# The routing's logits, taken from the transposed rows as stationary operand

## The chip, the core and the metric

The kernel runs on one core of a Trainium2 chip, as one program. The metric is the device time of the whole program in microseconds (us); the median of three runs is given with the lowest and the highest. PE is the TensorE matmul engine, PEld its loads of the stationary operand, DVE is VectorE, ACT is ScalarE, POOL is GpSimd, SP is SyncE.

## What is computed

Three stages follow one another; only the second contains the change. B = 4 batches, H = 8 heads, 768 positions, head dimension 48, so 3072 tokens of 384 numbers.

```
# 1 linear attention with a decaying state, per batch and head
for t in range(S):
    cur = einsum('bhd,bhe->bhde', u * k_t, v_t)
    y[:, :, t] = einsum('bhd,bhde->bhe', r_t, state + cur)
    state = w * state + einsum('bhd,bhe->bhde', k_t, v_t)
# 2 a mixture of 8 experts, each token goes to one
xn = x / (norm(x) + 1e-6);  en = emb / (norm(emb) + 1e-6)
logits = xn @ en.T / tau
e = argmax(logits);  gate = softmax(logits)[e]
out[mask_e] = gate * (relu(x[mask_e] @ w1[e]) @ w2[e])      # 384 -> 1024 -> 384
# 3 a dense feed-forward over all tokens, 384 -> 2048 -> 384
h = x @ w_in;  out = (h * clip(h + 3, 0, 6) / 6) @ w_out
```

## The kernel before

**Attention.** The sequence is cut into six chunks c of 128 positions, and the heads into four pairs hp. The loop runs over the 24 groups (c, hp), all four batches in each. In one group DVE scales the transposed r and k by tables (`r_s` L625, `k_s` L624), PE forms the scores `a_ps` (L632), ACT copies them to `a_m` and POOL masks them (L636). POOL also forms `ku`, the product of r, k and u (L640, L641); DVE sums it to `a_t` (L648) and multiplies v by it (`av`, L663). `kk` (L652) feeds `u_ps` (L660), from which DVE updates the state (L686). `y_ps` (L667, L671) is copied to `y_sb` and transposed back into `x_ps` (L690), and DVE adds `av` and writes the token rows `x_t` (L691). `x_t` has two buffers of 128 positions x 4 batches x 388, one per chunk; so chunk 5 writes the buffer from which chunk 3 was scattered.

**Routing.** `route(c)` treats the 512 tokens of a chunk once `x_t` is whole. It is a generator in four steps, taken one or two at a time between the groups of the next chunk. In step one, 12 transposes (L223) and three copies on ACT make `xT`, the rows with the 384 numbers on the partitions, and ACT sums the squares (L228). In step two, three matmuls (L233) have the normalised expert directions `enT` as stationary operand (8 columns, padded to 32 per block of 128) and 512 tokens moving; ACT copies `lt_ps` to `lt`. `inv_norm` (L201 to L214, 14 short DVE instructions) gives 1/norm. In step three, four transposes (L240) bring the logits back to one token per partition; DVE sums the three blocks (L242), takes the maximum (L245), subtracts it (L246), finds the first index at the maximum (L248 to L251), forms the one-hot `ohot` and `aft` (L254, L256), scales by 1/norm (L257), and ACT takes the exponential `ex` (L259). In step four, PE counts with triangular and all-ones matrices (`r_ps`, `c_ps`, L263 to L271), DVE reads the rank (L273, L275), the destination `dsti` (L277), the gate (L279 to L281, written into column 384 of `x_t`) and the running counts (L282, L283); POOL then issues four indirect scatters (L286), each of 128 rows of `x_t` to `xs_d` in memory.

All of the routing's PSUM tiles, and those of the experts' transposes, share one pool `psM` with two buffers. After chunk 2, `leader` (L339 to L349, with L325 as its last instruction) picks the expert with most tokens so far; its first 256 rows are gathered from `xs_d` (L385), and its weights are split into high and low parts (L189, L192).

**After the attention.** The expert with most tokens runs first. The routing of chunk 5 stands among its matmuls (L410 to L412, `mm3`) in an order fixed by `pin = tc.keep_in_program_order`. Its scatters, the final order of the experts and the gathers of the other experts follow. Everywhere else the order on an engine is not written out: a scheduler of the framework places instructions by its own model of when their inputs are ready. An engine runs its instructions strictly in the order so found.

Of the kernel before, what the change touches and what calls it, by code (L numbers as in the profile page):

```python
# [8 lines left out]
F32 = mybir.dt.float32  # L9
# [6 lines left out]
ALU = mybir.AluOpType  # L16
AX = mybir.AxisListType
# [4 lines left out]
B, H, S, D = 4, 8, 768, 48  # L22
NT = B * S
DM = H * D
KD = DM // 128
E, F1, F2 = 8, 1024, 2048
# [18 lines left out]
def rwkv_moe_kernel(ctx, tc, dT, tokA, wT, uw, emb, tau, w1, w2, win, wout, out):  # L45
    nc = tc.nc
    wide = win.dtype == I64

    const = ctx.enter_context(tc.tile_pool(name="const", bufs=1))
# [5 lines left out]
    psM = pctx.enter_context(tc.tile_pool(name="psM", bufs=2, space=PSUM))  # L55
# [12 lines left out]
    ident = const.tile([128, 128], F32, name="ident")  # L68
# [32 lines left out]
    start = const.tile([128, E], F32, name="start")  # L101
# [17 lines left out]
    lead_f = const.tile([128, 4], F32, name="lead_f")  # L119
    lead_i = const.tile([128, 2], I32, name="lead_i")  # L120
    n0 = lead_f[:, 1:2]
    enT = const.tile([128, KD, 32], F32, name="enT")
    nc.gpsimd.memset(enT, 0.0)


    w_src = []
# [82 lines left out]
    def inv_norm(pool, ss, shape, nm):  # L209

        y = rsqrt_newton(pool, ss, shape, nm)
        nc.vector.tensor_tensor(out=y, in0=y, in1=ss, op=ALU.mult)
        nc.vector.tensor_scalar(out=y, in0=y, scalar1=1e-6, scalar2=None, op0=ALU.add)
        nc.vector.reciprocal(out=y, in_=y)  # L214
        return y

    def route(c, x_t, sm, xT, st_p, group="rows", pin=lambda i: i):
# [10 lines left out]
            nc.scalar.activation(out=junk, in_=x_t[:, b, 0:DM], func=AF.Square, accum_out=ss[:, b:b + 1])  # L228
        yield

        lt_ps = psM.tile([KD * 32, B, 128], F32, name="lt_ps", tag="m")
        for k in range(KD):
            pin(nc.tensor.matmul(lt_ps[k * 32:k * 32 + 32], lhsT=enT[:, k, :], rhs=xT[:, k], start=True, stop=True))  # L233
        lt = sm.tile([KD * 32, B, 128], F32, name="lt", tag="lt")
        nc.scalar.copy(out=lt, in_=lt_ps)
        rn = inv_norm(sm, ss, [128, B], "n")
        yield
        l_ps = psM.tile([128, B, KD, 32], F32, name="l_ps", tag="m")
        for b in range(B):
            pin(nc.tensor.transpose(l_ps[:, b].rearrange("p k e -> p (k e)"), lt[:, b, :], ident[0:KD * 32, 0:KD * 32]))  # L240
        lg = sm.tile([128, B, E], F32, name="lg", tag="lg")
        nc.vector.tensor_reduce(out=lg, in_=l_ps[:, :, :, 0:E].rearrange("p b k e -> p b e k"), axis=AX.X, op=ALU.add)  # L242

        mx = sm.tile([128, B], F32, name="mx", tag="mx")
        nc.vector.tensor_reduce(out=mx, in_=lg, axis=AX.X, op=ALU.max)  # L245
        nc.vector.tensor_tensor(out=lg, in0=lg, in1=mx.unsqueeze(2).to_broadcast([128, B, E]), op=ALU.subtract)  # L246
        sel = sm.tile([128, B, E], F32, name="sel", tag="sel")
        nc.vector.tensor_scalar(out=sel, in0=lg, scalar1=0.0, scalar2=float(E), op0=ALU.is_lt, op1=ALU.mult)  # L248
        nc.vector.tensor_tensor(out=sel, in0=sel, in1=iot, op=ALU.add)
# [276 lines left out]
    with actx:  # L526
# [3 lines left out]
        sm = actx.enter_context(tc.tile_pool(name="sm", bufs=2))  # L530
# [43 lines left out]
        while n < C:  # L574
            nc.vector.tensor_tensor(out=ptab[:, :, n + 1:2 * n + 1], in0=ptab[:, :, 1:n + 1],
                                    in1=ptab[:, :, n:n + 1].to_broadcast([112, HP, n]), op=ALU.mult)
# [22 lines left out]
        def directions():  # L599

            emj = st_p.tile([128, DM], BF16, name="junk", tag="junk")[0:E, :]
            ess = st_p.tile([E, 1], F32, name="ess")
            nc.scalar.activation(out=emj, in_=em, func=AF.Square, accum_out=ess)
            ern = inv_norm(st_p, ess, [E, 1], "e")
            nc.vector.reciprocal(out=ta, in_=ta)
            nc.vector.tensor_scalar(out=em, in0=em, scalar1=ern, scalar2=ta, op0=ALU.mult, op1=ALU.mult)
            eps = psM.tile([128, KD, E], F32, name="eps", tag="m")
            for k in range(KD):
                nc.tensor.transpose(eps[:, k, :], em[:, k * 128:(k + 1) * 128], ident[0:E, 0:E])
            nc.vector.tensor_copy(enT[:, :, 0:E], eps)  # L610

        state = []
        for hp in range(HP):
# [91 lines left out]
        for i, (c, hp) in enumerate(groups):  # L705
# [9 lines left out]
            if i == 1:  # L715
                directions()
            if i == HP:
                range_flag()
            if hp == HP - 1 and c < NCH - 1:
                pend = route(c, x_t, sm, xp.tile([128, KD, B, 128], F32, name="xT", tag="xT", bufs=1), st_p)  # L720
# [21 lines left out]
        psC = pctx.enter_context(tc.tile_pool(name="psC", bufs=1, space=PSUM))  # L742
        pin = tc.keep_in_program_order
        last_r = route(NCH - 1, x_t, sm, xp.tile([128, KD, B, 128], F32, name="xT", tag="xT", bufs=1), st_p, pin=pin)
        step(last_r, 1)

# [133 lines left out]
    with ExitStack() as mctx:  # L880
        m1 = mctx.enter_context(tc.tile_pool(name="m1", bufs=1))

        def again():
# [44 lines left out]
            for c in range(NCH):  # L928
                x_t = m1.tile([128, B, DG], F32, name="x_t", tag="x")
                xT = stg.tile([128, WCH], F32, name="xT", tag="wst").rearrange("p (k b t) -> p k b t", k=KD, b=B)  # L930
                nc.gpsimd.memset(x_t[:, :, DM + 1:DG], 0.0)
                nc.sync.dma_start(out=x_t[:, :, 0:DM], in_=y_d.rearrange("(b c p) d -> c p b d", b=B, p=C)[c])
                for f in step(route(c, x_t, m1, xT, m1, "rows_again"), 4):
                    f()
# [208 lines left out]
```

## Time and profile before

| | us |
|---|---|
| median of 3 runs (lowest, highest) | 876.92 (872.75, 880.08) |
| the profiled execution | 870.2 |
| its span, first to last instruction | 868.5 |
| PE busy | 820.0 |
| DVE busy | 523.3 |
| ACT busy | 347.3 |
| POOL busy | 262.7 |

The mean granted TensorE clock of the profiled execution is 0.944 of full speed. Busy times are sums over the whole span; the engines run side by side. The attention with the routing of chunks 0 to 4 takes the first 200 us, the first expert with the routing of chunk 5 follows, and all after that is expert and feed-forward work. "Idle before" in a row is the time an engine stood still before the instruction, with what ended it. The granted clock is given as a share of 2.4 GHz, 0.50 being 1.2 GHz.

### The profile page before, as it was taken

To read this page: it belongs to the slowest core of one execution; us is meant where nothing else is said; L and a number is where in the kernel's file an instruction comes from. 1 tells how busy PE (TensorE), PEld (TensorE's weight loads), DVE (VectorE), ACT (ScalarE), POOL (GpSimd) and SP (SyncE) were. 2 spreads that over 40 slices of the span, in tenths; PEclk is the share of its full clock that TensorE was granted. 3 is DMA by queue.
4 is the path that set the end of the run, shared out by engine and by line. 5 is a ranking of instruction groups with operands and counts; after the bars stand their busy time and mean duration, and the time that the engine had idled before them with its cause. 6 is when DMAs were issued, how large, how long until landed. Compare 5 with 4: busy or idle time off the path is not lost. (4 is left out here: it accounts for less than half of the span.)

```text
span 868.5 us, 13312 instructions
## 1 busy us (share of the span) xinstructions
PE 820.0 (94%) x5005; PEld 729.0 (84%) x5006; DVE 523.3 (60%) x1105; ACT 347.3 (40%) x668; POOL 262.7 (30%) x280
## 2 busy tenths in 40 slices
PE   7998997979999999997898999999999999999994
PEld 5876785758899999997888888898998899988983
DVE  8478989977387877782546888744334334333331
ACT  3443343543544554452544433343333334333331
POOL 7646656755323322647210211121002002001001
PEclk8587888899999999999899999999999999999997
DMA  7434536713465656562222221111001001001001
GB/s 219 146 130 157 173 131 207 263 65 119 151 215 173 204 180 208 189 197 81 94 93 61 69 66 62 37 37 37 1 1 37 0 1 37 1 1 37 0 1 37
DMA packets 25083, 85.09 MB, mean 98 GB/s; under 512 B 4780, under 2 KB 7009, under 8 KB 25008
## 3 DMA queue, kind: packets, MB, share of 16 engines
q1 hardware_dynamic: 19072, 69.44, 24.9%
q0 software_dynamic: 5936, 14.70, 4.8%
q8 instruction: 42, 0.69, 0.3%
q14 instruction: 33, 0.27, 0.1%
HBM read 71.47 MB, written 12.64 MB: 97 GB/s over the span
## 5 line engine op out<-in xcount | busy, mean ns | idle before, releaser
L410 PE MATMUL l<-xh,whi 128*128 128x512 f32 (+8 forms) x504 | 184.9, 372 | 4.1 <-DVEq L1009 3.1
L411 PE MATMUL l<-xl,whi 128*128 128x512 f32 (+8 forms) x504 | 187.1, 372 | 1.2 <-issue 1.2
L412 PE MATMUL l<-xh,wlo 128*128 128x512 f32 (+8 forms) x504 | 186.6, 371 | 0.9 <-issue 0.9
L446 DVE SCALAR_TENSOR_TENSOR rg<-rg,l 128x512 f32<-128x512 f32 x96 | 65.7, 686 | 132.7 <-ACT rg L445 125.2
L445 ACT ACTIVATE rg<-l,three 128x512 f32<-128x512 f32 x96 | 65.8, 689 | 166.4 <-PE l L412 154.9
L461 PE MATMUL o<-wlo,hh 128*128 128x384 f32 x384 | 128.6, 335 | 0.4 <-POOL wlo L1039 0.4
L460 PE MATMUL o<-whi,hh 128*128 128x384 f32 x384 | 128.0, 336 | 0.5 <-ACT hh L447 0.5
L462 PE MATMUL o<-whi,hl 128*128 128x384 f32 x384 | 124.2, 335 | 0.0
L412 PEld LDWEIGHTS l<-xh,wlo 128*128 128x128 f32 x504 | 95.8, 190 | 15.1 <-issue 2.2
L410 PEld LDWEIGHTS l<-xh,whi 128*128 128x128 f32 x504 | 95.3, 190 | 15.2 <-issue 4.7
L411 PEld LDWEIGHTS l<-xl,whi 128*128 128x128 f32 x504 | 95.6, 190 | 11.3 <-issue 1.1
L1069 POOL DMA_INDIRECT out_dram<-o_t,ctok x20 | 20.9, 1043 | 254.1 <-ACT o_t L1067 250.5
L448 DVE TENSOR_TENSOR hl<-rg,hh 128x512 fp32r<-128x512 f32 x96 | 66.4, 693 | 43.5 <-ACT hh L447 42.1
L447 ACT CAST hh<-rg 128x512 fp32r<-128x512 f32 x96 | 59.5, 621 | 75.1 <-DVE rg L446 60.4
L507 DVE SCALAR_TENSOR_TENSOR hl<-l,hh 128x256 fp32r<-128x256 f32 (+7 forms) x72 | 38.1, 541 | 69.7 <-ACT hh L506 53.8
L460 PEld LDWEIGHTS o<-whi,hh 128*128 128x128 f32 x384 | 72.0, 188 | 5.2 <-ACT hh L447 0.8
L461 PEld LDWEIGHTS o<-wlo,hh 128*128 128x128 f32 x384 | 72.1, 188 | 4.3 <-POOL wlo L1039 0.7
L506 ACT ACTIVATE hh<-l 128x256 fp32r<-128x256 f32 (+7 forms) x72 | 33.6, 481 | 103.2 <-PE l L412 63.3
L411 PE MATMUL acc<-hl,whi 128*128 128x256 f32 (+7 forms) x216 | 72.0, 335 | 0.5 <-issue 0.2
L412 PE MATMUL acc<-hh,wlo 128*128 128x256 f32 (+7 forms) x216 | 72.4, 336 | 0.0
L462 PEld LDWEIGHTS o<-whi,hl 128*128 128x128 f32 x384 | 71.7, 188 | 0.3
L410 PE MATMUL acc<-hh,whi 128*128 128x256 f32 (+7 forms) x216 | 65.1, 335 | 0.1
(216 smaller groups left out, 1332.6 us busy)
## 6 DMA issues: line engine op xcount, KB each, us to landing
wst<-in_w_dram SPq DMA_DIRECT2D x32, 768.0 KB
tk<-in_tok_dram SPq DMA_DIRECT2D x24, 576.0 KB
dt_t<-in_dT_dram SPq DMA_DIRECT2D x24, 448.0 KB
q<-in_win_dram SPq DMA_DIRECT2D x16, 384.0 KB
q<-in_wout_dram SPq DMA_DIRECT2D x16, 384.0 KB
wf_d<-t SPq DMA_DIRECT2D x16, 192.0 KB
wst<-wf_d SPq DMA_DIRECT2D x4, 768.0 KB
rows<-xs_d,prod POOLq DMA_INDIRECT x27
```

Source lines behind the costliest of these rows:

```text
L410: pin(nc.tensor.matmul(ps, lhsT=w[0], rhs=x[0], start=first, stop=False))
L411: pin(nc.tensor.matmul(ps, lhsT=w[0], rhs=x[1], start=False, stop=False))
L412: pin(nc.tensor.matmul(ps, lhsT=w[1], rhs=x[0], start=False, stop=last))
L445: nc.scalar.activation(out=r6, in_=ps, func=AF.Relu, bias=three)
L446: nc.vector.scalar_tensor_tensor(out=gf, in0=r6, scalar=6.0, in1=ps, op0=ALU.min, op1=ALU.mult)
L447: nc.scalar.copy(out=gh, in_=gf)
L448: nc.vector.tensor_tensor(out=gl, in0=gf, in1=gh.bitcast(F32), op=ALU.subtract)
L460: pin(nc.tensor.matmul(acc[t], lhsT=gh[:, sl], rhs=wh[:, f % 4, :], start=(f == span[0]), stop=False))
L461: pin(nc.tensor.matmul(acc[t], lhsT=gh[:, sl], rhs=wl[:, f % 4, :], start=False, stop=False))
L462: pin(nc.tensor.matmul(acc[t], lhsT=gl[:, sl], rhs=wh[:, f % 4, :], start=False, stop=(f == span[1] - 1)))
L506: last["a"] = nc.scalar.activation(out=hh[:, 0:n], in_=ps[:, 0:n], func=AF.Relu).ins
L507: last["v"] = nc.vector.scalar_tensor_tensor(out=hl[:, 0:n], in0=ps[:, 0:n], scalar=0.0, in1=hh[:, 0:n].bitcast(F32), op0=ALU.max, op1=ALU ...
```

## The change

`enT` loses its padding and is [128, 3, 8]; the memset of the padded tile goes. In step two of `route`, the logits are formed by 12 matmuls per chunk: for each batch b and each block k of 128 numbers, `xT[:, k, b]` (128 x 128) is the stationary operand and `enT[:, k]` (8 columns) moves; the three blocks add up in PSUM. `l_ps` therefore has tokens on the partitions at once. The three matmuls L233, the copy to `lt`, the four transposes L240 and the sum L242 are gone. The maximum and the subtraction read `l_ps` from PSUM and stand at the end of step two, ahead of `inv_norm` in the program. What follows is as before. Line numbers in the text are those of before; those of the changed file are 7 lower from L246 on (1 lower in `inv_norm`), and its own maximum and subtraction are L236 and L237.

```diff
--- before.py
+++ after.py
@@ -119,8 +119,7 @@
     lead_f = const.tile([128, 4], F32, name="lead_f")
     lead_i = const.tile([128, 2], I32, name="lead_i")
     n0 = lead_f[:, 1:2]
-    enT = const.tile([128, KD, 32], F32, name="enT")
-    nc.gpsimd.memset(enT, 0.0)
+    enT = const.tile([128, KD, E], F32, name="enT")
 
 
     w_src = []
@@ -228,22 +227,16 @@
             nc.scalar.activation(out=junk, in_=x_t[:, b, 0:DM], func=AF.Square, accum_out=ss[:, b:b + 1])
         yield
 
-        lt_ps = psM.tile([KD * 32, B, 128], F32, name="lt_ps", tag="m")
-        for k in range(KD):
-            pin(nc.tensor.matmul(lt_ps[k * 32:k * 32 + 32], lhsT=enT[:, k, :], rhs=xT[:, k], start=True, stop=True))
-        lt = sm.tile([KD * 32, B, 128], F32, name="lt", tag="lt")
-        nc.scalar.copy(out=lt, in_=lt_ps)
+        l_ps = psM.tile([128, B, E], F32, name="l_ps", tag="m")
+        for b in range(B):
+            for k in range(KD):
+                pin(nc.tensor.matmul(l_ps[:, b], lhsT=xT[:, k, b], rhs=enT[:, k], start=(k == 0), stop=(k == KD - 1), skip_group_check=True))
+        lg = sm.tile([128, B, E], F32, name="lg", tag="lg")
+        mx = sm.tile([128, B], F32, name="mx", tag="mx")
+        nc.vector.tensor_reduce(out=mx, in_=l_ps, axis=AX.X, op=ALU.max)
+        nc.vector.tensor_tensor(out=lg, in0=l_ps, in1=mx.unsqueeze(2).to_broadcast([128, B, E]), op=ALU.subtract)
         rn = inv_norm(sm, ss, [128, B], "n")
         yield
-        l_ps = psM.tile([128, B, KD, 32], F32, name="l_ps", tag="m")
-        for b in range(B):
-            pin(nc.tensor.transpose(l_ps[:, b].rearrange("p k e -> p (k e)"), lt[:, b, :], ident[0:KD * 32, 0:KD * 32]))
-        lg = sm.tile([128, B, E], F32, name="lg", tag="lg")
-        nc.vector.tensor_reduce(out=lg, in_=l_ps[:, :, :, 0:E].rearrange("p b k e -> p b e k"), axis=AX.X, op=ALU.add)
-
-        mx = sm.tile([128, B], F32, name="mx", tag="mx")
-        nc.vector.tensor_reduce(out=mx, in_=lg, axis=AX.X, op=ALU.max)
-        nc.vector.tensor_tensor(out=lg, in0=lg, in1=mx.unsqueeze(2).to_broadcast([128, B, E]), op=ALU.subtract)
         sel = sm.tile([128, B, E], F32, name="sel", tag="sel")
         nc.vector.tensor_scalar(out=sel, in0=lg, scalar1=0.0, scalar2=float(E), op0=ALU.is_lt, op1=ALU.mult)
         nc.vector.tensor_tensor(out=sel, in0=sel, in1=iot, op=ALU.add)
@@ -607,7 +600,7 @@
             eps = psM.tile([128, KD, E], F32, name="eps", tag="m")
             for k in range(KD):
                 nc.tensor.transpose(eps[:, k, :], em[:, k * 128:(k + 1) * 128], ident[0:E, 0:E])
-            nc.vector.tensor_copy(enT[:, :, 0:E], eps)
+            nc.vector.tensor_copy(enT, eps)
 
         state = []
         for hp in range(HP):
```

The scheduler places the attention's instructions anew. Three places follow, before and after, with the line numbers of each file.

On POOL, at the end of the attention: `ku` is the product that DVE's `a_t` sums, `a_m` the mask, the DMA rows the scatters of a chunk. Before:

```order
L640 TENSOR_TENSOR ku<-tk,ubc 128x384
L641 TENSOR_TENSOR ku<-ku,tk 128x384
L640 TENSOR_TENSOR ku<-tk,ubc 128x384
L636 AFFINE_SELECT a_m<-a_m 128x512 x2
L641 TENSOR_TENSOR ku<-ku,tk 128x384
L286 DMA xs_d<-x_t,dsti 3072x388 x4
L636 AFFINE_SELECT a_m<-a_m 128x512 x2
L711 MEMSET x_t 128x4x3
```

The scatters are those of chunk 3; the `ku` products of the last two groups of the attention (two multiplications each) stand ahead of them. After:

```order
L634 TENSOR_TENSOR ku<-ku,tk 128x384
L279 DMA xs_d<-x_t,dsti 3072x388 x4
L633 TENSOR_TENSOR ku<-tk,ubc 128x384
L629 AFFINE_SELECT a_m<-a_m 128x512 x2
L634 TENSOR_TENSOR ku<-ku,tk 128x384
L704 MEMSET x_t 128x4x3
L633 TENSOR_TENSOR ku<-tk,ubc 128x384
L629 AFFINE_SELECT a_m<-a_m 128x512
L634 TENSOR_TENSOR ku<-ku,tk 128x384
L629 AFFINE_SELECT a_m<-a_m 128x512
L633 TENSOR_TENSOR ku<-tk,ubc 128x384
L634 TENSOR_TENSOR ku<-ku,tk 128x384
```

The scatters of chunk 3 now stand ahead of the `ku` products of the last three groups.

On DVE, the same chunk 3 between its gate and its destination rows. Before:

```order
L691 TENSOR_TENSOR x_t<-x_ps,av 128x4x96
L648 TENSOR_REDUCE a_t<-ku 128x8
L279 TENSOR_REDUCE gate<-ex 128x4
L663 TENSOR_TENSOR av<-tk,a_t 128x384
L280 TENSOR_SCALAR gate<-gate 128x4
L281 RECIPROCAL x_t<-gate 128x4
L648 TENSOR_REDUCE a_t<-ku 128x8
L273 TENSOR_TENSOR at<-r_ps,ohot 128x32
L282 TENSOR_TENSOR cum<-c_ps,cum 128x8
L283 TENSOR_TENSOR delta<-c_ps,cum 128x8
L275 TENSOR_REDUCE rank<-at 128x4
L277 TENSOR_SCALAR dsti<-rank 128x4
```

Here the gate (L279 to L281) stands ahead of `dsti` (L277), with the two last `a_t` of the attention among them. After, from `dsti` on:

```order
L270 TENSOR_SCALAR dsti<-rank 128x4
L641 TENSOR_REDUCE a_t<-ku 128x8
L273 TENSOR_SCALAR gate<-gate 128x4
L274 RECIPROCAL x_t<-gate 128x4
L617 TENSOR_TENSOR k_s<-dt_t,itab 112x512
L684 TENSOR_TENSOR x_t<-x_ps,av 128x4x96
L679 SCALAR_TENSOR_TENSOR state_0_229<-state_1_230,ptab,u_ps 48x4x48 x2
L656 TENSOR_TENSOR av<-tk,a_t 128x384
L618 TENSOR_TENSOR r_s<-dt_t,ptab 112x512
L641 TENSOR_REDUCE a_t<-ku 128x8
L684 TENSOR_TENSOR x_t<-x_ps,av 128x4x96
L617 TENSOR_TENSOR k_s<-dt_t,itab 112x512
```

Behind `dsti` (now L270) and the reciprocal (now L274, the other input of the scatters) stand `k_s`, `x_t`, two state updates, `av` and `r_s`, and then an `a_t` whose `ku` is behind the scatters on POOL.

On DVE, chunk 0, the first scatters. Before, from the reciprocal on, which there stands behind `dsti`:

```order
L281 RECIPROCAL x_t<-gate 128x4
L624 TENSOR_TENSOR k_s<-dt_t,itab 112x512
L691 TENSOR_TENSOR x_t<-x_ps,av 128x4x96
L686 SCALAR_TENSOR_TENSOR state_0_224<-state_1_225,ptab,u_ps 48x4x48 x2
L652 TENSOR_TENSOR kk<-tk,ktab 128x384
L663 TENSOR_TENSOR av<-tk,a_t 128x384
L625 TENSOR_TENSOR r_s<-dt_t,ptab 112x512
```

Twenty instructions lie between this reciprocal and the next `a_t` that needs a `ku` from behind the scatters. After, from `dsti` on, which here stands behind the reciprocal:

```order
L270 TENSOR_SCALAR dsti<-rank 128x4
L618 TENSOR_TENSOR r_s<-dt_t,ptab 112x512 x2
L684 TENSOR_TENSOR x_t<-x_ps,av 128x4x96
L656 TENSOR_TENSOR av<-tk,a_t 128x384
L617 TENSOR_TENSOR k_s<-dt_t,itab 112x512
L679 SCALAR_TENSOR_TENSOR state_1_230<-state_0_229,ptab,u_ps 48x4x48 x2
L645 TENSOR_TENSOR kk<-tk,ktab 128x384
L641 TENSOR_REDUCE a_t<-ku 128x8
```

The `a_t` is now the ninth instruction after `dsti` (`x2` counts as two), the routing's own instructions for chunk 1 no longer lying between.

## Rows read from the trace of the kernel before

**Rows 1.** page, part 1: engine, busy us (share of the span), instructions

```profile
PE 820.0 (94%) x5005; PEld 729.0 (84%) x5006; DVE 523.3 (60%) x1105; ACT 347.3 (40%) x668; POOL 262.7 (30%) x280
```

**Rows 2.** windows: length; PE, PEld, DVE, ACT, POOL busy; PEclk, DMA, GB/s

```profile
75.00:80.00 5.00, 5.00 (x41) 3.76 (x37) 3.58 (x11) 2.10 (x5) 2.00 (x2) 0.50 0.39 144
150.00:155.00 5.00, 5.00 (x34) 3.69 (x34) 4.01 (x13) 3.58 (x8) 0.00 (x0) 0.50 1.04 359
165.00:170.00 5.00, 4.18 (x48) 3.42 (x46) 4.99 (x10) 2.57 (x5) 5.00 (x4) 1.00 0.79 253
320.00:868.00 548.00, 524.28 (x2685) 479.43 (x2684) 279.59 (x483) 207.88 (x362) 100.20 (x90) 0.98 0.18 56
```

**Rows 3.** groups by form, DVE, 45-195 us: busy, mean ns | idle, releaser

```profile
L625 DVE TENSOR_TENSOR r_s<-dt_t,ptab 112x512 f32<-112x512 f32 x18 | 15.8, 879 | 0.5 <-PE y_ps L667 0.4
L624 DVE TENSOR_TENSOR k_s<-dt_t,itab 112x512 f32<-112x512 f32 x17 | 15.0, 880 | 4.7 <-issue 3.5 <-PE a_ps L632 1.2
L686 DVE SCALAR_TENSOR_TENSOR state<-state,ptab,u_ps 48x192 f32<-48x192 f32 x32 | 13.1, 410 | 4.1 <-PE u_ps L660 3.8
L663 DVE TENSOR_TENSOR av<-tk,a_t 128x384 f32<-128x384 f32 x20 | 12.8, 642 | 0.0
L691 DVE TENSOR_TENSOR x_t<-x_ps,av 128x384 f32<-128x384 f32 x22 | 12.2, 554 | 7.2 <-DMA xs_d<-x_t,dsti 4.0 <-PE x_ps L690 2.7
L652 DVE TENSOR_TENSOR kk<-tk,ktab 128x384 f32<-128x384 f32 x17 | 11.4, 677 | 0.9 <-DMA tk<-in_tok_dram 0.5 <-PE u_ps L660 0.2
L648 DVE TENSOR_REDUCE a_t<-ku 128x8 f32<-128x384 f32 x19 | 10.3, 543 | 0.1
L325 DVE TENSOR_SCALAR ix<-lead_f 128x2 int32<-128x2 f32 x1 | 6.0, 5950 | 0.0
L242 DVE TENSOR_REDUCE lg<-l_ps 128x32 f32<-128x96 f32 x5 | 1.2, 248 | 0.0
```

**Rows 4.** groups by form, PE, 50 to 205 us, same columns

```profile
L233 PE MATMUL lt_ps<-xT,enT 128*32 128x512 f32 x36 | 11.8, 666 | 0.3 <-issue 0.3
L240 PE MATMUL l_ps<-ident,lt 96*128 96x96 f32 x24 | 3.2, 255 | 0.4 <-ACT lt L235 0.4
```

**Rows 5.** timeline, PE: start, us, engine, line, op, [idle before <-releaser]

```profile
42.92 0.48 PE L609 MATMUL eps<-ident,em 8*128 8x8 f32 x3
43.33 0.45 PE L586 MATMUL kps<-ident,kt_d 112*128 112x112 f32 x1
...
92.19 0.53 PE L660 MATMUL u_ps<-tk,kk 128*48 128x48 f32 x16
92.65 1.13 PE L667 MATMUL y_ps<-r_s,state 112*112 112x128 f32 x8
```

**Rows 6.** timeline, POOL, the scatters of chunk 0

```profile
77.69 1.16 POOL L286 DMA_INDIRECT xs_d<-x_t,dsti  x1 [4.55 <-DVE x_t L281]
...
82.79 1.02 POOL L640 TENSOR_TENSOR ku<-tk,ubc 128x384 f32<-128x384 f32 x1
83.74 1.23 POOL L636 TENSOR_SCALAR_AFFINE_SELECT a_m<-a_m 128x512 f32<-128x512 f32 x2
84.93 1.00 POOL L641 TENSOR_TENSOR ku<-ku,tk 128x384 f32<-128x384 f32 x1
```

**Rows 7.** timeline, DVE, the last group row of the attention

```profile
188.94 0.56 DVE L691 TENSOR_TENSOR x_t<-x_ps,av 128x384 f32<-128x384 f32 x1 [4.03 <-DMA xs_d<-x_t,dsti]
```

**Rows 8.** timeline, PE, ahead of the slices from 75 us

```profile
73.97 0.66 PE L223 MATMUL t_ps<-ident,x_t 128*128 128x128 f32 x4 [2.63 <-DVE at L273]
```

**Rows 9.** waits, DVE, 15 to 198 us: sum, times, longest

```profile
DVE a_t L648 <- POOL ku L641: 1.0, 1, 1.0
```

**Rows 10.** timeline, PE, the rank matmuls of chunk 5

```profile
204.11 0.19 PE L263 MATMUL r_ps<-ohot,tri 128*128 128x32 bf16 x1 [0.60 <-DVE ohot L254]
```

**Rows 11.** timeline, DVE and ACT, the routing of chunk 4

```profile
191.58 0.18 DVE L257 TENSOR_TENSOR lg<-lg,ny 128x32 f32<-128x32 f32 x1
192.07 0.25 ACT L259 ACTIVATE ex<-lg 128x32 f32<-128x32 f32 x1
```

## The prediction

> **What bounds the kernel now.** I read the page first: over the whole span PE is busy 94%, DVE 60%, ACT 40% [rows 1]. That is an average over two unlike stages, so the table by stretch comes next. From 320 us to the end PE is busy 524.28 of 548 us [rows 2]; that is expert and feed-forward work which the diff doesn't touch. The edited helper `route` runs in the first 205 us, in and just behind the attention, and there the bound changes hands. In the stretch 165 to 170, DVE is busy 4.99 of 5 us while PE has gaps at full clock; in 75 to 80, PE is busy all the time at a granted clock of 0.50 (the 1.2 GHz level) while DVE has 1.4 us free [rows 2]. Before that fall of the clock, PE stood idle for 2.63 us [rows 8]. So in this stage a microsecond taken from DVE counts while DVE is full, one taken from PE counts at the low clock, and one taken from ACT counts only through a wait. A microsecond won before the first expert matmul is a microsecond of the end, because PE's work follows on from there.
>
> **The change, part by part.** Everything is priced in the profiled execution: 870.2 us on the device, of which 868.5 is the span. The median of the runs shown, 876.92, is 6.7 above it; I add that at the end.
>
> *PE.* Removed per chunk: three matmuls of 512 columns and four transposes. Over the six chunks they keep PE busy 11.8 and 3.2 us [rows 4], 15.0 together. Added per chunk: 12 matmuls, each with a stationary operand of 128 columns and 8 columns moving. An fp32 matmul leaves two records (the 18 of L233 are counted x36), so 24 records per chunk, 144 in all. No row has this very shape. The nearest is L609, which loads 128 columns and moves 8: three from 42.92 to 43.33, that is 137 ns each at clock 0.50, 68 ns at full clock [rows 5]. From below: u_ps, with 48 columns on both sides, passes 16 records from 92.19 to 92.65, 29 ns each. From above: L667, 112 stationary and 128 moving columns, 8 in 1.13 us, 141 ns each [rows 5]. I take 68, since the load is the same and the moving part nothing: 144 x 0.068 = 9.8 us. PE gains 5.2 us over the program, between a gain of 10.8 (4.2 added) and a loss of 5.3 (20.3 added). Most of it lies beside DVE's full stretches and is worth nothing; in the short stretches at the low clock I count 0.5 us, and keep -1 to +2 for the range.
>
> That L609 row is the one which a page of the Trainium skill disputes. TensorE: Matmul & The Clock Gate, section "LDWEIGHTS (loading the stationary operand)", has the load cost the number of columns divided by 1.2, in ns, however few the rows: 107 ns for 128 columns. By it, an estimate from that page, 144 records would cost 15.4 us, PE would gain nothing, and the sum below would be 0.5 us higher. The row at half clock is slower than that, its half faster, so the trace doesn't settle it.
>
> *ACT.* The copy of lt goes, and with it the place in ACT's queue where a_m and y_sb copies stood behind lt_ps. ACT is 40% busy; it is priced at nothing, and hidden by DVE and PE.
>
> *DVE.* The sum over three column groups, L242, goes: 248 ns [rows 3], five times before the first expert, -1.2 us. The maximum and the subtraction stay, now from PSUM. In the new order gate (L279) stands directly behind the product lg (L257) in three chunks, with ACT's exp between them. In the trace lg ends at 191.76 and exp at 192.32 [rows 11], so DVE would wait about 0.6 each time, 1.7 in all; two of the three lead into a longer wait on POOL below. I count +0.5, from 0 to +1.7.
>
> *What moves.* The shorter chain lets the scheduler place each chunk's routing earlier among the attention groups, and this is the larger effect. The pieces of order above show it for chunk 3. Before, its four row scatters stood on POOL behind every ku of the attention; now they stand ahead of the ku products of the last three groups. On DVE the instruction that needs the next ku is a_t, and in the old order a_t never stood behind scatters not yet done: DVE's wait for ku sums to 1.0 us [rows 9].
>
> Price: from the first scatter to the end of the ku behind it, chunk 0 took 77.69 to 85.93, 8.24 us [rows 6]: four scatters, ku, two a_m, ku. The new order behind chunk 3 holds the same. Between L281, which releases the scatters, and that a_t, DVE now has k_s, x_t, two state, av and r_s: 0.88 + 0.55 + 0.82 + 0.64 + 0.88 = 3.8 us [rows 3]. So DVE stands **4.4 us** at a_t, with k_s and r_s of the last groups queued behind it, and PE's a_ps behind those. For chunk 0 DVE has two r_s, x_t, av, k_s, two state and kk, 5.3 us: a wait of 2.9. For chunk 1, twelve instructions (three kk and av, five k_s, r_s and x_t, four state and, first, one a_t) of 7.4 us against 8.9 with one more a_m: 1.5. Chunk 2 has 8.6 against 8.2, no wait. The waits of chunks 0 and 1 come where PE ran at the low clock before (75 to 80), DVE having time to spare there; I count half of them, 2.2, and keep 0 and 4.4. The one of chunk 3 has no such cover.
>
> What goes in return: x_t of the last group row waited 4.03 us for chunk 3's scatters to land before its buffer could be written [rows 7]. In the new order that x_t stands some 12 us of DVE work behind the same scatters, so **-4.0**. What is late next is a_t, above: one wait takes the place of the other.
>
> *Behind the attention.* Chunk 5's r_ps waited 0.60 us on PE for ohot [rows 10]. Without copy, transposes and sum its ohot comes sooner, and PE arrives with 1.6 us of logits in place of about 1.5: -0.5. Scatter, gather and the next expert's first matmul follow from there.
>
> *L325.* One instruction of two elements took 5.95 us [rows 3], at the end of chunk 2, behind four scatters and the POOL work after them. It stands at the same place in the new order. If it is held again, nothing changes; if it runs like L242's 0.25, 5.7 us are won. Its place says held: -0.5.
>
> **Sum:** -1.2 - 4.0 - 0.5 - 0.5 - 0.5 + 4.4 + 2.2 + 0.5 = **+0.4**: 870.6 on the profiled execution, **877** as a median.
>
> **Rivals.** *Faster:* L325 isn't held (-5.2 beyond the sum), and with the last chunk's r_ps no longer late PE skips the 2.63 us idle ahead of the low clock at 75 [rows 8]. Two slices of 5 us at half clock cost 5 us of PE work. 877.3 - 5.2 - 5.0 = 867. For it: the 2.63 us idle waited for `at` of chunk 0, which comes some 4 us sooner. Against: the 2.9 us wait stands in the same place.
> *Slower, by one mechanism:* DVE at a_t behind the scatters. If nothing covers chunks 0 and 1, +2.2; and if PE, starved of k_s and r_s, idles there and behind chunk 3 as long as it did before 75, two more stretches like 75 to 85 cost 5 each: 877.3 + 2.2 + 10 = 889.5. For it: DVE is full at 165. It decides from the second such stretch on; one makes 884.5, still inside 1%.
> *The change doesn't do what it says:* the logits on PE cost as much as what they replace (the load as the bound, 141 ns a record). That adds 0.5 to 2.5 us, 877 to 880, and ends in the likeliest case.
>
> **How the numbers follow.** A measurement of this kernel tells about 1%, 8.8 us, from no change. Within 1% (868.1 to 885.7), the likeliest with the third rival: 0.54. The faster rival, 0.25: two independent things, each near even, one of them on DVE's full stretch. The slower, 0.21. With the bounds of the terms (-2.2 and +2.2 for cover, -5.2 for L325, +2 for PE, +1.2 for exp) the likeliest alone spans 869 to 883; reaching to both rivals until a tenth is left out on each side gives 865 to 888.
>
> **What would show it.** Right, if in the new profile DVE a_t waits on POOL ku for 6 us or more in total, if the wait of x_t on its own scatters is gone, and if L233 keeps PE busy near 10 us. Wrong, if a_t doesn't wait (POOL's scatters are then cheaper than 8.2), if L325 is short, if L233 exceeds 15 us, or if the stretches at clock 0.50, two of which are in [rows 2], become more or fewer in the attention.

## The result and the profile after

Over 20 runs of each, the changed kernel takes 874.43 us in the median (868.98 to 883.98), the kernel before 873.20 (865.29 to 884.61). The ratio is **1.0069**, 95% interval 1.0042 to 1.0095. That is 6 us, and less than 1%: on the scale of the prediction, no change. The ratio compares fast runs alone, those within 1.5% of the fastest of their kernel; the medians of all 20 lie only 1.2 us apart. Later the kernel before was timed against itself, on another chip, and gave 0.9953 (0.9920 to 0.9985), and the changed kernel there 0.9998 (0.9958 to 1.0039). So sets of runs differ by half a per cent with nothing changed, and the size of the loss is not known better than that.

The profiled execution of the changed kernel takes 872.3 us, 870.6 of it the span. First the page, part 1, of the changed kernel, to be held beside [rows 1]:

```profile
PE 824.9 (95%) x5089; PEld 746.4 (86%) x5090; DVE 517.6 (59%) x1099; ACT 342.9 (39%) x662; POOL 261.6 (30%) x279
```

Then its groups by form, DVE, 45 to 200 us (columns as in [rows 3]): the sum `a_t`, and the clamp that was L325.

```profile
L641 DVE TENSOR_REDUCE a_t<-ku 128x8 f32<-128x384 f32 x19 | 10.4, 548 | 17.0 <-POOL ku L634 11.5 <-POOL x_t L704 5.5
L318 DVE TENSOR_SCALAR ix<-lead_f 128x2 int32<-128x2 f32 x1 | 0.2, 170 | 0.0
```

`a_t` stood idle for 17.0 us before its instructions, where it was 0.1 [rows 3]; the wait of `x_t` on its own scatters [rows 7] is in no row any more. The clamp took 0.17 us, not 5.95. On PE, groups by form, 45 to 215 us:

```profile
L233 PE MATMUL l_ps<-enT,xT 128*128 128x8 f32 x144 | 21.4, 283 | 0.0
```

The 12 logits matmuls per chunk kept PE busy for 21.4 us, where the two lines they replace had 15.0 [rows 4].

The wait that the prediction put at 4.4 us is this one, timeline of the changed kernel, POOL, DVE and PE:

```profile
164.65 1.25 POOL L279 DMA_INDIRECT xs_d<-x_t,dsti  x1 [2.48 <-DVE x_t L274]
...
168.82 0.98 POOL L279 DMA_INDIRECT xs_d<-x_t,dsti  x1 [0.30 <-issue]
169.81 1.01 POOL L633 TENSOR_TENSOR ku<-tk,ubc 128x384 f32<-128x384 f32 x1
170.76 1.23 POOL L629 TENSOR_SCALAR_AFFINE_SELECT a_m<-a_m 128x512 f32<-128x512 f32 x2
...
171.95 1.00 POOL L634 TENSOR_TENSOR ku<-ku,tk 128x384 f32<-128x384 f32 x1
...
172.98 0.55 DVE L641 TENSOR_REDUCE a_t<-ku 128x8 f32<-128x384 f32 x1 [5.49 <-POOL x_t L704]
...
177.86 0.71 PE L625 MATMUL a_ps<-r_s,k_s 48*128 48x128 f32 x8 [2.26 <-DVE r_s L618]
```

The four scatters of chunk 3 run from 164.65 to 169.80, then ku, two a_m, ku, as in chunk 0 before [rows 6]. The `a_t` behind them waited 5.49 us (the row names the memset that follows the ku on POOL), and some 5 us later PE waited 2.26 for `r_s`. The windows of the changed kernel (columns as in [rows 2]) show what came next:

```profile
175.00:180.00 5.00, 2.74 (x29) 2.00 (x28) 5.00 (x6) 2.66 (x9) 3.72 (x4) 0.98 0.24 95
180.00:185.00 5.00, 5.00 (x26) 4.56 (x22) 4.40 (x19) 0.91 (x2) 1.23 (x2) 0.50 0.00 0
```

PE is busy 2.74 of 5 us, and then the clock is 0.50. The first expert matmul starts at 199.7 us, where it was 197.5. From there to the end it is 670.9 us now and 671.0 before. In this pair of profiles the whole 2.1 us lie in the attention.

### The profile page after: what moved, and what is told of

It is laid out like the page before. It is cut to its first block, busy times and chain, and to the rows that moved or that the text cites. A ratio compares the mean times of both kernels' runs of the same rounds, so it can differ in the third digit from the quotient of the medians.

```text
span 870.6 us, 13458 instructions
## 1 busy us (share of the span) xinstructions
PE 824.9 (95%) x5089; PEld 746.4 (86%) x5090; DVE 517.6 (59%) x1099; ACT 342.9 (39%) x662; POOL 261.6 (30%) x279
## 5 line engine op out<-in xcount | busy, mean ns | idle before, releaser
L438 ACT ACTIVATE rg<-l,three 128x512 f32<-128x512 f32 x96 | 65.8, 690 | 172.7 <-PE l L405 162.7
```

The source lines that it names most:

```text
L438: nc.scalar.activation(out=r6, in_=ps, func=AF.Relu, bias=three)
```

## What was tried on the chip

Two theories. **A:** the loss is DVE's waits for `ku` behind scatters. **B:** it is PE's: the logits cost more there than was counted, and PE is the bound. All ratios below are to the kernel before, run on the same chip.

**Chunk 3's scatters behind every ku.** A third buffer for `x_t`, so that its writes needn't wait for them, and an order on POOL: `HOLD` names the group from which on a chunk's scatters may be issued, and `behind` puts each behind the last `ku` written so far. In the traces nothing else moves but one `a_t`, by one place. (`...` marks lines left out.)

```diff
+HOLD = {3: 24}
...
+            if c in HOLD:
+                behind(sc, "ku")
...
-                x_t = xp.tile([128, B, DG], F32, name="x_t", tag="x", bufs=2)
+                x_t = xp.tile([128, B, DG], F32, name="x_t", tag="x", bufs=3)
...
-                rest.pop(0)()
+                if i + 2 >= HOLD.get(first, 0):
+                    rest.pop(0)()
```

> The changed kernel with a third x_t buffer, and chunk 3's four scatters put behind the last ku of the attention on POOL, as they stood in the kernel before; nothing else moves. In the changed kernel DVE's a_t waited 5.49 us at 172.98 us for the ku behind these scatters. Theory A (the waits of a_t behind the scatters make the loss): that wait is gone, the first expert matmul starts 4 to 6 us earlier than 199.7 us, and the ratio to the kernel before is 1.000 to 1.003 where the changed kernel has 1.0069. Theory B (the loss is PE's own: logits 21.4 us busy where 15.0 were before): the wait goes but the time stays, ratio 1.005 to 1.009.

Its control, the third buffer alone:

> The changed kernel with a third x_t buffer alone, the order on every engine as in the changed kernel: the control for the run with ku ahead of the scatters. In the changed kernel no x_t waits for scatters to land, so both theories expect its ratio to the kernel before to be that of the changed kernel, 1.004 to 1.010, and a_t to wait for POOL 12 to 17 us in all.

Measured: 1.0007 (0.9965 to 1.0049) against 1.0081 (1.0038 to 1.0124) for the control. That looked like theory A. The difference is hardly wider than the two intervals, so the pair was run once more, with the changed kernel as it is and the kernel before in the place of an edited one.

> The changed kernel itself, beside the kernel with ku ahead of the scatters, on one chip. If the loss belongs to the kernel and not to a set of runs: ratio 1.004 to 1.010 (it was 1.0069, and 1.0081 with a third buffer); a_t waits 5 to 6 us behind the scatters of chunk 3. If sets of runs differ by as much as this: anything from 0.998 to 1.004.

> The same kernel as in the first run with chunk 3's scatters behind the last ku. Theory A: 0.5 to 1.0% under the changed kernel measured beside it, as the first time (1.0007 against 1.0081), and a trace of an undisturbed run in which no a_t between 160 and 190 us waits over 3 us. Theory B: within 0.3% of the changed kernel.

> The kernel before, timed against itself, in the place of an edited kernel: shows what a difference of nothing looks like. 0.997 to 1.003 if the intervals hold; the two runs that left the 5 us hold in place and moved no other order gave 0.9934 and 1.0009. In its trace the clamp L325 takes 5 to 6 us if the hold belongs to the order, 0.2 if it comes and goes between executions.

Measured: the changed kernel 0.9998 (0.9958 to 1.0039), the one with ku ahead 1.0107 (1.0069 to 1.0146), the kernel before against itself 0.9953. The order of the first pair is turned round. The wait itself did go, as the DVE waits, 15 to 215 us, of the second run of ku ahead show (sum, times, longest):

```profile
DVE a_t L645 <- POOL ku L637: 12.1, 10, 2.4
```

Nothing over 2.4 us is left, and 12.1 in all where it was 17.0; yet the first expert matmul starts at 198.7 us, beside 199.7 in the changed kernel and 196.3 in the control; 4 to 6 us ahead of 199.7 were expected. **Theory A falls:** a wait of 5.5 us was taken away and no time came back. The two pairs of times contradict each other, so the difference of the first is put down to the scatter of the runs.

**The scatters of chunks 0 to 3 all behind ku products.** The same edit with `HOLD = {0: 10, 1: 14, 2: 17, 3: 24}`. In the trace the scatters of chunks 0 and 1 stand one and two `ku` products later, in pairs; the four of chunk 2 stand together behind the same product as in the changed kernel, against what was expected.

> The changed kernel with a third x_t buffer, and the scatters of chunks 0 to 3 all put behind ku products, those of chunks 0 to 2 in pairs with a ku between, those of chunk 3 behind the last ku as in the run before. Theory A (a_t's waits behind scatters are the loss, at every chunk): a_t waits for POOL under 6 us in all where it was 17, and the ratio is 0.994 to 0.999, below that of the run with chunk 3 alone (1.0007). Theory B (what is left is PE's): the waits shrink and the ratio stays at 1.000 to 1.004.

Measured: 1.0031 (0.9975 to 1.0086), and of the waits (DVE, 15 to 215 us):

```profile
DVE a_t L645 <- POOL ku L637: 9.4, 5, 3.0
```

9.4 us, where under 6 were expected. The ratio lies in the range of theory B, with an interval that reaches into that of A. It speaks against A and proves nothing for B.

**The logits twice.**

```diff
-        for b in range(B):
+        for b in [b for b in range(B) for _ in range(2)]:
             for k in range(KD):
```

> The changed kernel with each token block's three logits matmuls issued twice (the second pass starts the sum again): 144 more records on PE. 24 records took 2.82 us at full clock and 20 took 4.44 us at half clock, so L233 should be busy 34 to 43 us. Theory A (PE's part is mostly beside DVE's waits): the time rises by 2 to 9 us over the changed kernel, ratio to the kernel before 1.009 to 1.017. Theory B (PE's logits are on the path): it rises by 17 to 21 us, ratio 1.026 to 1.031. The order of the attention shifts a little with it, so a few us either way are not told apart.

Measured: 1.0487 (1.0429 to 1.0545), far over both. Groups by form, PE, 45 to 240 us, and DVE waits, 15 to 235 us:

```profile
L233 PE MATMUL l_ps<-enT,xT 128*128 128x8 f32 x288 | 48.1, 307 | 0.0
```

```profile
DVE mx L236 <- PE l_ps L233: 14.3, 4, 6.2
```

The records cost 167 ns each in place of 118 to 149, since more of them ran at the low clock, and DVE waited 14.3 us for the logits, where it had waited 0.4. The order moved with it, so 36 us over the changed kernel is no price of 144 records. It shows the logits on the path when they are doubled; that they are on it as the changed kernel has them is argued from this, not shown. Theory B is the one that is left.

**The clamp in other forms, in the kernel before.** Two runs on why L325 took 5.95 us. First with both inputs from memory (`scalar_tensor_tensor`), then as a reduce over the sum and the bound laid side by side in the work tile.

```diff
-        nc.vector.tensor_scalar(out=ix, in0=r, scalar1=float(n * B * C - 1), scalar2=None, op0=ALU.min)
+        nc.vector.scalar_tensor_tensor(out=ix, in0=r, scalar=float(n * B * C - 1), in1=r, op0=ALU.min, op1=ALU.min)
```

```diff
-        nc.vector.tensor_tensor(out=r, in0=r, in1=pos, op=ALU.add)
-        nc.vector.tensor_scalar(out=ix, in0=r, scalar1=float(n * B * C - 1), scalar2=None, op0=ALU.min)
+        cl = wrk[:, 240:240 + 2 * t].rearrange("p (t x) -> p t x", x=2)
+        nc.vector.memset(cl[:, :, 1:2], float(n * B * C - 1))
+        nc.vector.tensor_tensor(out=cl[:, :, 0:1], in0=r.unsqueeze(2), in1=pos.unsqueeze(2), op=ALU.add)
+        nc.vector.tensor_reduce(out=ix, in_=cl, axis=AX.X, op=ALU.min)
```

> The kernel before with one instruction in another form: the clamp L325, which held DVE for 5.95 us while POOL ran from 140.09 to 145.35 us without a gap, is a scalar_tensor_tensor with the row sum on both inputs (same value). In the changed kernel the clamp took 0.17 us, beside POOL's scatters. If the hold comes with the form of the instruction: 0.2 us, and the time falls by 3 to 6 us, ratio 0.993 to 0.997. If any DVE instruction there is held while POOL computes: 5 to 6 us again and ratio 0.998 to 1.002.

> The kernel before with the clamp L325 as a reduce: the bound is written beside the row sum in the work tile and the smaller of the two is taken, one input in place of two or of a scalar form; two short memsets are added on DVE and no other order moves. With L325 as a scalar_tensor_tensor the hold stayed at 5.35 us (and the times were 0.9934 of the kernel before). If the hold belongs to the form (the inputs it reads while POOL computes): under 0.5 us, the first expert starts 3 to 6 us earlier, ratio 0.993 to 0.997. If any instruction there is held while POOL runs without a gap: 5 to 6 us again, and a ratio of 0.998 to 1.002 if that of the other form was the scatter of the runs.

Measured: 0.9934 (0.9891 to 0.9977) and 1.0009 (0.9969 to 1.0049). The first profile has the hold unchanged, timeline, DVE:

```profile
139.43 5.35 DVE L325 SCALAR_TENSOR_TENSOR ix<-lead_f 128x2 int32<-128x2 f32 x1
```

so its ratio is no gain of the form; it is about what the kernel before showed against itself. In the second the reduce is short and the hold is on the next instruction, timeline, DVE and POOL:

```profile
139.73 0.15 DVE L327 TENSOR_REDUCE ix<-wrk 128x2 int32<-128x4 f32 x1
139.85 5.24 DVE L347 CAST lead_i<-lead_f 128x2 int32<-128x2 f32 x1
140.39 1.01 POOL L642 TENSOR_TENSOR ku<-tk,ubc 128x384 f32<-128x384 f32 x1
...
144.07 0.98 POOL L642 TENSOR_TENSOR ku<-tk,ubc 128x384 f32<-128x384 f32 x1
...
145.02 0.62 POOL L638 TENSOR_SCALAR_AFFINE_SELECT a_m<-a_m 128x512 f32<-128x512 f32 x1
```

The copy L347 begins while POOL still scatters, and lasts until near the end of POOL's row of ku and a_m. And in the kernel before, run against itself with nothing edited, the clamp took 0.48 us, where 5 to 6 were expected if the hold belonged to the order; there the hold fell on an instruction shortly ahead of it (timeline, DVE and POOL):

```profile
131.89 5.15 DVE L343 TENSOR_TENSOR key<-lead,cum 128x8 f32<-128x8 f32 x1
132.35 1.01 POOL L640 TENSOR_TENSOR ku<-tk,ubc 128x384 f32<-128x384 f32 x1
...
137.16 0.48 DVE L325 TENSOR_SCALAR ix<-lead_f 128x2 int32<-128x2 f32 x1
```

So the hold belongs neither to the instruction nor to the order, but to the moment: in all four profiles it meets an instruction that DVE begins during the last scatter, 0.46 to 0.67 us ahead of a stretch in which POOL computes without a gap. In the changed kernel DVE passes the clamp at 129.42, and POOL is then issuing scatters (timeline, POOL, of the changed kernel):

```profile
127.98 1.39 POOL L279 DMA_INDIRECT xs_d<-x_t,dsti  x1 [2.42 <-DVE wrk L304]
129.68 0.99 POOL L279 DMA_INDIRECT xs_d<-x_t,dsti  x1 [0.30 <-issue]
```

**Logits in eight rows.** A third form, without loads of the transposed rows: `enT` stationary as before, the three blocks summed in PSUM, a copy of 8 rows, four transposes, and maximum and subtraction from PSUM.

```diff
+        lt_ps = psM.tile([E, B, 128], F32, name="lt_ps", tag="m")
+        for k in range(KD):
+            pin(nc.tensor.matmul(lt_ps, lhsT=enT[:, k, :], rhs=xT[:, k], start=(k == 0), stop=(k == KD - 1)))
+        lt = sm.tile([E, B, 128], F32, name="lt", tag="lt")
+        nc.scalar.copy(out=lt, in_=lt_ps)
...
+            pin(nc.tensor.transpose(l_ps[:, b], lt[:, b, :], ident[0:E, 0:E]))
```

> A third form of the logits: expert directions stationary as in the kernel before, but the three blocks summed in PSUM into 8 rows, copied, and transposed back by four transposes; no sum on DVE, and no load of the transposed rows. On PE per chunk at full clock some 2.0 us for the three matmuls and 0.3 for the transposes, against 2.5 before and 2.85 in the changed kernel. The scatters of chunk 3 stand behind every ku. Theory A: no a_t wait above 3 us there, ratio 0.993 to 1.000. Theory B, with 3.3 us less PE than the changed kernel at full clock and up to 8 at the low clock: ratio 0.996 to 1.001. If the ratio is above 1.004, neither holds.

With the scatters behind ku besides, in two sets of runs:

> The eight-row logits with a third x_t buffer and the scatters of chunks 0 to 3 behind ku products. Theory A: a_t and x_t wait for no scatter, the best of all, ratio 0.988 to 0.996. Theory B: as the eight-row form alone, within 0.003.

> The eight-row logits with the scatters behind ku products, again (0.9962, interval up to 0.9999): 0.993 to 0.999 if it beats both kernels, 1.000 to 1.003 if the first time was scatter.

Measured: 1.0047 (1.0005 to 1.0088) alone; with ku ahead 0.9962 (0.9925 to 0.9999), and again 1.0016 (0.9982 to 1.0049). The first misses both theories, the second pair says that nothing was gained over the kernel before. No version tried beats both kernels.

## Where the attention's time went: the clock

The profiles of these runs, read side by side, show what the times alone could not. The row to read is the mean granted clock from 50 us to the first expert matmul (windows; columns as in [rows 2]; the first row of each is 20 to 50 us). The kernel before, as profiled for the prediction, and in the run against itself:

```profile
20.00:50.00 30.00, 30.00 (x187) 25.62 (x186) 16.21 (x33) 10.95 (x22) 17.00 (x22) 0.50 0.33 106
50.00:197.50 147.50, 131.80 (x1320) 101.00 (x1318) 125.27 (x332) 63.59 (x145) 92.83 (x99) 0.87 0.49 166
```

```profile
20.00:50.00 30.00, 29.93 (x272) 25.18 (x272) 19.53 (x40) 15.09 (x34) 20.42 (x24) 0.73 0.47 146
50.00:189.30 139.30, 120.54 (x1236) 92.37 (x1236) 122.93 (x326) 59.04 (x133) 91.59 (x98) 0.90 0.50 167
```

The changed kernel, and the one with ku ahead:

```profile
20.00:50.00 30.00, 30.00 (x272) 25.31 (x270) 23.27 (x41) 15.46 (x36) 19.31 (x23) 0.73 0.46 144
50.00:199.70 149.70, 135.24 (x1306) 115.21 (x1304) 112.85 (x321) 54.07 (x123) 90.23 (x97) 0.79 0.49 159
```

```profile
20.00:50.00 30.00, 30.00 (x270) 25.30 (x270) 20.60 (x40) 15.29 (x34) 19.86 (x24) 0.72 0.45 146
50.00:198.70 148.70, 133.29 (x1305) 113.66 (x1304) 112.63 (x321) 54.07 (x124) 91.74 (x96) 0.79 0.48 161
```

| profile | clock 20 to 50 us | clock 50 us to first expert | first expert at, us |
|---|---|---|---|
| before | 0.50 | 0.87 | 197.5 |
| before, clamp as reduce | 0.50 | 0.88 | 197.2 |
| scatters of all chunks behind ku | 0.50 | 0.82 | 207.7 |
| before, against itself | 0.73 | 0.90 | 189.3 |
| changed | 0.73 | 0.79 | 199.7 |
| changed, third buffer | 0.74 | 0.80 | 196.3 |
| ku ahead, second run | 0.72 | 0.79 | 198.7 |

Two things are in it. In the first 50 us the clock rises early in some executions and late in others, with either kernel, and that moves everything behind it by some 8 us (197.5 and 189.3 for the kernel before). The two profiles of the prediction and of the result happen to differ in it: before had the late rise, after the early one. **Like with like, the attention is 7 to 11 us longer** with the new logits (189.3 against 196.3 to 199.7, and 197.2 against 207.7). The second of these pairs has moved scatters besides; a later profile of the changed kernel as it is, also with the late rise, has its first expert at 209.2 us and a clock of 0.79 behind 50 us, and the first one of ku ahead has 209.1. Each of these differences is more than the 6 us of the 20 runs, and the second set of runs gave none. How often the clock rises early in the executions that were timed and not profiled is not known; that may be why. From the first expert to the end the seven profiles take between 659.6 and 675.0 us, with either kernel, so that some of the loss may come back there. In the four with the early rise most of it stays: their spans are 864.3 us for the kernel before, and 870.6, 871.0 and 872.7 with the new logits.

And the clock of the attention is lower with the new logits in each profile, 0.79 to 0.82 for 0.87 to 0.90. A fall in the changed kernel, timeline, PE, and windows of 1 us:

```profile
50.52 2.85 PE L233 MATMUL l_ps<-enT,xT 128*128 128x8 f32 x24
```

```profile
52.00:53.00 1.00, 1.00 (x11) 1.00 (x11) 1.00 (x4) 0.00 (x0) 0.00 (x0) 1.00 0.09 37
53.00:54.00 1.00, 1.00 (x22) 0.98 (x23) 1.00 (x3) 0.00 (x0) 0.74 (x1) 0.73 0.00 0
54.00:55.00 1.00, 1.00 (x15) 0.93 (x10) 0.93 (x3) 0.00 (x0) 0.92 (x2) 0.50 0.76 229
```

PE was busy without a gap, 24 records of loads with 8 columns moving behind them, and the granted clock went from 1.00 to 0.50 as the block ended. The old form in the kernel before, three matmuls with 512 columns moving, began at 57.0 us; windows behind it:

```profile
58.00:59.00 1.00, 1.00 (x31) 0.96 (x28) 1.00 (x3) 0.58 (x1) 1.00 (x1) 1.00 0.02 9
59.00:60.00 1.00, 1.00 (x13) 0.81 (x9) 1.00 (x4) 0.59 (x1) 1.00 (x2) 1.00 0.00 0
```

The clock stayed. Counted over the four profiles with the new logits in the table: 19 blocks of 20 to 26 records began at full clock, and in 15 the clock fell during the block or within 1.4 us of its end, with PE idle for at most 0.6 us in the 5 us ahead (a stretch taken for this count only). The three profiles of the kernel before in the table have 16 falls between 40 and 215 us; 15 came behind 1.1 us of idle time or more, and the one other (102.0 us, PE without a gap) about a microsecond behind chunk 1's rank matmuls, which have 8 to 32 columns moving; none came within 6 us behind a block of the old logits. The three profiles with eight rows have twelve falls, all behind idle time of 0.9 us or more and none within 4 us behind their logits, and in the one alone the attention has:

```profile
50.00:194.50 144.50, 129.31 (x1320) 96.17 (x1319) 122.78 (x327) 63.92 (x146) 91.05 (x98) 0.92 0.51 169
```

So the falls behind the blocks are shown. What in a block does it, the many loads or the few columns moving, no run tells apart. What it costs is worked out: at 0.79 for 149.7 us, 42% of the time or 63 us were at 1.2 GHz, at 0.87 for 147.5 us 38; 25 us more at half speed are 12 us of PE's work. Like with like it is more: the kernel before against itself has 0.90 for 139.3 us, 28 us at 1.2 GHz, so 35 us more and some 17 us of PE's work. Against these stand the gains on DVE. This is an estimate; no run took the falls away and kept the rest.

## Why the prediction was right, and where it was not

The time lies in the range, near its middle, and the direction (no change over 1%) is right. Some of that is luck. The forecast stands on a median of three runs, 876.92, where 20 runs gave 873.20; so 874.43 lies under the forecast of 877 although the loss (1.2 us by the medians, 6 by the ratio) is larger than the +0.4 that was counted. Three of the signs that it gave for being wrong are there, though: L233 over 15 us, L325 short, more stretches at 0.50. In the sum two errors of opposite sign met: the clamp's 5.8 us were not counted as a gain, and the cost of the logits and of the clock behind them not as a loss.

**PE, the step that failed.** The step: "I take 68, since the load is the same and the moving part nothing". L609 loads and moves as many columns, but it is of another kind: transposes, one record each, of 8 rows. At full clock 24 records took 2.82 us (200.82 to 203.64 us), 118 ns each: 17.0 us for 144, where 9.8 were counted. The two lines removed kept PE busy for 15.0 us, and for 13.6 with each block weighed by its granted clock. So at full clock PE loses 3.4 us, and in the two profiles 6.4; it doesn't gain 5.2. Of the two rows that gave the bounds, the upper one (L667, 141 ns, real matmuls with 112 columns loaded) was the near one. The estimate from the Trainium skill, TensorE: Matmul & The Clock Gate, section "LDWEIGHTS (loading the stationary operand)", 107 ns for 128 columns, was 9% low; the row which it disputed was 42% low. The remaining 4.4 of the 21.4 us are the blocks that ran at the low clock.

**The clock, named only as a rival.** The slower rival had PE starved behind `a_t` and falling; it allowed two more such stretches. The clock did fall more often, eight times between 40 and 215 us where the kernel before had four; one fall came behind PE's wait of 2.26 us for `r_s`, as that rival has it, but half of the eight came with PE idle for at most 0.24 of the 5 us ahead, behind the logits themselves. No term of the sum held that. Its price, 12 to 17 us by the working above, is what can have used up the gain on DVE; the runs show the falls, and the price is only worked out.

**The a_t waits, about right in size behind chunks 0, 1 and 3, wrong in total and in weight.** Forecast: 2.9 us behind chunk 0's scatters, 1.5 behind chunk 1's, none at chunk 2, 4.4 at chunk 3. Measured: 2.45, 1.49, 2.44, 5.49, and five smaller ones besides, 17.0 in all for the 8.8 forecast. But "the one of chunk 3 has no such cover" was wrong in effect: with it taken away nothing came back. It wasn't that PE ran at the low clock there, for in the changed kernel the clock around that wait was 1.00 (windows):

```profile
163.00:179.00 16.00, 12.53 (x128) 10.15 (x126) 10.33 (x19) 7.12 (x17) 12.17 (x15) 1.00 0.45 152
```

With ku ahead the low clock in front of that place lasted from 142.4 to 166.3 us, where the changed kernel had it from 149.0 to 162.7; that can have taken what the wait gave, and no run shows it.

**The DMA wait of x_t, -4.0:** gone as forecast, and in the kernels with ku ahead the third buffer kept it away. **L242, -1.2, and the copy:** gone; DVE's busy time from 50 us to the first expert fell from 125.27 to 112.85 us, 5.8 of it the clamp. L242's own 1.2 us did not stay won: the product with 1/norm that follows (L257, 182 ns) took 486 ns in the mean, 1.5 us more over five chunks.

**Behind the attention, -0.5:** chunk 5's `r_ps` no longer waited, but it started later, 8.6 us behind the first expert matmul where it had been 6.6. The logits there took 2.82 us, where the old matmuls and transposes had 1.06 and 0.50, and behind them the clock fell, at 203.65 us; until 207.06 the expert's matmuls followed one another at 0.21 us in place of 0.12 (timeline, PE, changed kernel):

```profile
200.82 2.82 PE L233 MATMUL l_ps<-enT,xT 128*128 128x8 f32 x24
...
208.32 0.19 PE L256 MATMUL r_ps<-ohot,tri 128*128 128x32 bf16 x1
```

**L325, -0.5 in place of -5.8.** "Its place says held" read the order, and the clamp's neighbours on DVE were the same. What decides is when: DVE came there 10 us earlier, while POOL was between its first two scatters; and in the kernel before, run once more, the clamp took 0.48 us and its neighbour the hold. The Trainium skill's SBUF — State Buffer, section "SBUF: two separate sides", has VectorE (with two inputs from SBUF, or in a mode that uses two ports) and GpSimd shut each other out for a whole instruction. The rows agree that one shuts the other out; but 5.15 to 5.95 us were a row of seven POOL instructions, not one, and in the kernel before, between 45 and 195 us, 18 of 28 products of DVE (kk, av, k_s, r_s and wlo) that lay beside POOL's computing took their usual 0.54 to 0.9 us, the others up to 1.5.

**The gate behind exp, +0.5:** DVE's gate waited 1.3 us in three places; right within the range given, 0 to 1.7.

**The rivals.** The faster one's condition (L325 not held) came true, and its time didn't, because its second condition, no fall behind chunk 0, failed: the clock fell at 53.5 us, and at 67.1 behind 2.54 us of idle time, the like of the 2.63 before. The third, that logits on PE cost as much as what they replace, is nearest to what was found, and it left out the clock.

## What to carry to other kernels

Many loads of a full stationary operand with a handful of columns moving are priced by the load, from a row of real matmuls in the same form, and not from transposes; and the granted clock behind such a block is read too, since it may cost more than the block. A wait that is taken away need not come back as time: here 5.5 us on DVE did not. Before two profiles are subtracted, compare the clock in a part that the change doesn't touch: here a clock that rose 14 us later in one of them hid most of the difference.

## What was not expected of the hardware

The granted clock fell from 1.00 to 0.50 in or just behind 15 of 19 blocks of 128-column loads with 8 columns moving, with PE idle for at most 0.6 of the 5 us ahead. An instruction of DVE on two to eight elements was held for 5.15 to 5.95 us until near the end of POOL's run of computing, in four forms; the same clamp in the same order took 5.95 us in one execution and 0.48 in another, where an instruction ahead of it was held. And the kernel before, timed against itself, gave 0.9953 with an interval that leaves out 1: intervals from some 12 runs on one chip are narrower than what separates two sets of runs.
